# Attention by hash bucket and a gated FFN on one core: one shared hash for two head pairs, another split of the norm's transposes, and one accumulator emptied earlier

## The chip, the cores and the metric

The kernel runs on 1 core of one Trainium2 chip. The metric is device time in microseconds (us). The five engines are TensorE (PE, with its weight loads shown apart as PEld), VectorE (DVE), ScalarE (ACT), GpSimd (POOL) and SyncE (SP), which here only issues DMAs. Each works through its own instructions in order; semaphores tie them together.

## What is computed

```python
def _attn_ref(q, k, v, proj):                      # (4, 8, 768, 64), proj (64, 6)
    q_bits = (np.einsum('bhsd,dk->bhsk', q, proj) > 0)
    k_bits = (np.einsum('bhsd,dk->bhsk', k, proj) > 0)
    q_bucket, k_bucket = ...                        # the 6 bits as one number
    mask = q_bucket[:, :, :, None] == k_bucket[:, :, None, :]
    scores = scale * np.matmul(q, k.transpose(0, 1, 3, 2))
    scores = np.where(mask, scores, -1000000000.0)
    attn = softmax(scores)                          # with 1e-9 added to the sum
    return np.matmul(attn, v)

def _moe_ref(x, w_gate, w_val, w_out, rms_g):       # x: 3072 tokens of 512, d_ff 1536
    xn = x / sqrt(mean(x * x) + 1e-06) * rms_g
    g = xn @ w_gate
    return (g * sigmoid(g) * (xn @ w_val)) @ w_out
```

A query sees only the keys whose six signs agree with its own. The result of the attention, with the heads side by side, goes through an RMS norm and a gated FFN.

## The kernel before

**Units.** The work is cut into 8 units: batch `b` and half of the queries, `u = 2 * b + half`, 384 queries each. A unit has attention for 8 heads, then norm, gate and value matmuls (12 blocks `ft` of the hidden width) and the projection. Heads are prepared in pairs `(b, hp)`, four per batch.

**The mask as rows of the scores.** A pair's q and k are turned so that the 64 dimensions lie on partitions. The hash multiplies them by the projection (`pj`, on PE, in fp32), DVE's `signs` turns the sign bit of each result into plus or minus a constant, and these 6 rows of bits stand below the 64 rows of q and k in the tile `QK` as rows 64 to 69, so that one matmul gives score plus matching term. `hash_direct` (L244) hashes one pair: `hash_pairs` (L230) puts its four sources (k and q of both heads) in four blocks of 32 rows of a bank, one bank for each half `e` of the 768 tokens, `sign` writes them to the tile `bits`, and `send` (L270) has SP copy 6 rows each into `QK` by DMA, four DMAs per pair. `hash_half` (L212) is the other form, used from pair (1, 2) on.

**Steps.** The order of the instructions on every engine is written by a loop over 192 steps `t` (L873 on): scores of step `t + 1` on PE, the exp `probs` of step `t` on ACT, then what `plan[t]` holds. A step is a third of one head. `order` (L590) says which unit and head: units 0 and 1 share the first 48 steps, then 24 steps for each unit. Three steps after its scores a head's weighted sum `av` (L362) runs in two steps; `s_ps` has two buffers, the accumulator `o_ps` of a head pair has one. When a pair of heads is done, `o_step` (`attn_out`, L378) adds the mean term into `otmp` on DVE, which empties `o_ps`, takes the reciprocal, and POOL multiplies into `x` and squares it; `s_step` sums the squares on DVE some steps later.

**Order inside a step.** What is put in with `at` while the loop over `order` runs comes first in its step. A unit's FFN work is spread over the next unit's 24 steps by `spread` (L790), a planner which fills steps by estimated costs (`TURN` 220, `FEED` 324, and so on); it comes after. The list `late` comes behind that. An `o_step` is in `late` unless it falls before step 48 or on place 2 or 4 of a unit's 24 steps.

**The norm.** `norm` (L442) scales the three 128-token thirds of `x` to `xn` in fp16. A third is then turned into `xnT`, either by PE (`turn_x`, L458: four transposes into the bank `x_ps`, then DVE or ACT multiplies by the gain column `gcol`) or by DMA (`turn_dma`, L424, issued by SP; then DVE has put in the gain, as the row `grow`, while scaling). `ONDMA` (L422) says how many thirds of each unit go by DMA. All small PE results (`t_ps`, `d_ps`, `m_ps`, `x_ps`, `g_ps`, `v_ps`, `y_ps`, `z_ps`) share three banks.

**Around the first norm.** Unit 0's last heads end at step 31; its norm, on DVE and POOL, runs in steps 31 to 37. Pair (1, 0) is hashed in step 26 and sent in step 28, pair (1, 1) in steps 32 and 38 (L739 to L743). Dummy matmuls `z_ps` stand in steps 34 to 36. SP has the block loads of pair (1, 2) (`load_blocks`, eight DMAs, and one of V) in step 34 of its queue; the weights come over POOL's queue.

**The tail.** Behind the loop (L883 on): unit 6's projection of thirds 0 and 1, unit 7's norm, the projection of third 2 with unit 7's three turns between its parts, then unit 7's gates, values and projection with nothing else left to overlap.

Of the kernel before, what the change touches and what calls it, by code (L numbers as in the profile page):

```python
# [8 lines left out]
FP32 = mybir.dt.float32  # L9
# [8 lines left out]
S = 768  # L18
D = 64
DMODEL = H * D  # L20
DFF = 1536
NF = DFF // 128
# [11 lines left out]
def kernel(  # L34
# [12 lines left out]
    nc = tc.nc  # L47
    PSUM = bass.MemoryType.PSUM

    const = ctx.enter_context(tc.tile_pool(name="const", bufs=1))  # L50
# [16 lines left out]
    ones_row = nc.const_aps.tensor(1.0, [128, 512], mybir.dt.bfloat16)  # L67
    ones_sq = nc.const_aps.tensor(1.0, [128, 128], mybir.dt.bfloat16)
    praw = const.tile([D, 6], FP32, name="praw")
    pj = const.tile([128, 38], FP32, name="pj")  # L70
    ebias = const.tile([128, 1], FP32, name="ebias")
    mhalf = const.tile([128, 3], FP32, name="mhalf")
    ssp = [const.tile([128, 5, 3], FP32, name=f"ssp{i}") for i in range(2)]
# [60 lines left out]
    KROWS = D + 6  # L134
    qT, kT, QK = {}, {}, {}
# [36 lines left out]
    def turned(b, hp, which):  # L172
        return (qT if which == "q" else kT)[b, hp].rearrange("p (h c) -> p h c", h=2)
# [38 lines left out]
    def hash_half(parts):  # L212

        ps = bank("d_ps", [128, HALF])
        for t, src in parts:
            nc.tensor.matmul(  # L216
                ps[32 * t : 32 * t + 32, :], pj[:, 0:32], src,
                start=True, stop=True, tile_position=(0, 32 * t),
            )
        return ps  # L220
# [6 lines left out]
            op0=ALU.bitwise_and, op1=ALU.bitwise_or,  # L227
        )

    def hash_pairs(srcs):  # L230


        pss = [bank("d_ps", [128, HALF]) for _ in range(2)]
        for t, src in enumerate(srcs):
            for e in range(2):
                nc.tensor.matmul(  # L236
                    pss[e][32 * t : 32 * t + 32, :],
                    pj[64 * e : 64 * e + 64, 6 * e : 6 * e + 32],
                    src[64 * e : 64 * e + 64],
                    start=True, stop=True, tile_position=(64 * e, 32 * t),  # L240
                )
        return pss

    def hash_direct(b, hp, heads):  # L244

        where = [(which, hh) for hh in heads for which in "kq"]
        pss = hash_pairs([turned(b, hp, which)[:, hh, :] for which, hh in where])
        bt = spool.tile([128, S], FP16, name="bits")  # L250

        def sign(e):
            signs(bt[:, e * HALF : (e + 1) * HALF], pss[e])

        def direct(which, e, c0=0, c1=HALF):
            t = where.index((which, heads[0]))
            o = (0 if which == "q" else S) + e * HALF
            signs(
                QK[b, 2 * hp + heads[0], "h"][D:KROWS, o + c0 : o + c1],
                pss[e][32 * t : 32 * t + 6, c0:c1],  # L260
            )

        def move(hh):
            for which in "kq":
                t, o = where.index((which, hh)), 0 if which == "q" else S
                nc.gpsimd.tensor_copy(
                    QK[b, 2 * hp + hh, "h"][D:KROWS, o : o + S], bt[32 * t : 32 * t + 6, :]
                )

        def send(only=heads):  # L270
            for t, (which, hh) in enumerate(where):
                if hh not in only:
                    continue
                o = 0 if which == "q" else S
                nc.sync.dma_start(
                    out=QK[b, 2 * hp + hh, "h"][D:KROWS, o : o + S],
                    in_=bt[32 * t : 32 * t + 6, :],
                )

        return sign, direct, move, send  # L280

    hashed = {}
# [136 lines left out]

    rstds = {}  # L420

    ONDMA = {2: 2, 3: 2, 4: 2, 5: 2, 6: 3}  # L422

    def turn_dma(u, c):  # L424
        if c == 0:
            xnT[u] = npool.tile([128, 4, HALF], FP16, name="xnT", bufs=2)
        nc.sync.dma_start_transpose(  # L427
            out=xnT[u][:, :, c * 128 : (c + 1) * 128], in_=xn[u][:, c, :]
        )
# [12 lines left out]
    def norm(u):  # L442
        if u not in rstds:
            norm_scale(u)
        xn[u] = npool.tile([128, 3, DMODEL], FP16, name="xn")
        for c in range(3 if u else 2):
            if c < ONDMA.get(u, 0):
                nc.vector.scalar_tensor_tensor(
                    out=xn[u][:, c, :], in0=x[u][:, c, :], scalar=rstds[u][:, c : c + 1],
                    in1=grow, op0=ALU.mult, op1=ALU.mult,  # L450
                )
            else:
                norm_third(u, c, nc.vector.tensor_scalar_mul)

    def norm_third(u, c, mul):
        mul(xn[u][:, c, :], x[u][:, c, :], rstds[u][:, c : c + 1])

    def turn_x(u, c, act=False):  # L458
        if c == 0:
            xnT[u] = npool.tile([128, 4, HALF], FP16, name="xnT", bufs=2)  # L460
        ps = bank("x_ps", [128, 4, 128], FP16)
        for kt in range(4):
            nc.tensor.transpose(ps[:, kt, :], xn[u][:, c, kt * 128 : (kt + 1) * 128], ident16)  # L463
        dst = xnT[u][:, :, c * 128 : (c + 1) * 128]
        if act:
            for kt in range(4):
                nc.scalar.mul(dst[:, kt], ps[:, kt], gcol[:, kt : kt + 1])
        else:
            nc.vector.tensor_mul(dst, ps, gcol.unsqueeze(2).to_broadcast([128, 4, 128]))
# [34 lines left out]
    def project(u, c, f0, f1):  # L504
        if f0 == 0:
            obank[u, c] = bank("y_ps")
        y = obank[u, c]
        for ft in range(f0, f1):
            nc.tensor.matmul(  # L509
                y, ht[u][:, ft, c * 128 : (c + 1) * 128], wo[:, ft, :],  # L510
                start=(ft == 0), stop=(ft == NF - 1),
            )
# [6 lines left out]
    def store(u, c):  # L519
        ysb = spool.tile([128, DMODEL], FP32, name="ysb", bufs=3)  # L520
        nc.scalar.copy(ysb, obank.pop((u, c)))  # L521
        nc.sync.dma_start(out=rows_of(u, c), in_=ysb)
# [39 lines left out]
    )  # L562
    for e in range(2):
        rows = slice(64 * e, 64 * e + 64)
        nc.gpsimd.tensor_scalar_mul(pj[rows, 6 * e : 6 * e + 6], praw, -1.0)
    for i in range(2):
        nc.gpsimd.memset(vls[i][:, :, :, 64:65], 1.0)
        nc.gpsimd.memset(vsum[i][:, :, 64:65], 6.0)
# [19 lines left out]
    NS = 24  # L588
# [5 lines left out]
    def at(w, s, f, *a):  # L594
        plan[NS * w + s].append(lambda: f(*a))
# [87 lines left out]
    for hp, ts in ((0, (8, 22, 23, 24, 25, 24, 39, 26, 28, 42)), (1, (20, 27, 28, 29, 30, 29, 41, 32, 33, 43))):  # L683
        tl, ts = ts[0], ts[1:]
        for w in "kq":
            at(0, tl, load_natural, nc.sync, 1, hp, w)
        at(0, tl, load_v, nc.sync, 1, hp)
        at(0, ts[0], new_pair, 1, hp)
        for t, hh, w in zip(ts[0:4], (0, 1, 0, 1), "kkqq"):
            at(0, t, turn_pe, 1, hp, hh, w)  # L690
        at(0, ts[4], cast_pool, 1, hp, "k")
        at(0, ts[5], cast_pool, 1, hp, "q")
        if hp == 0:
            at(0, ts[6], hash_pair, 1, hp)
            at(0, ts[7], send_pair, 1, hp)
        at(0, ts[8], v_prep, 1, hp)
        at(0, ts[8], v_sum, 1, hp)

# [14 lines left out]
    TX = 37  # L713
# [7 lines left out]
    def s_step(u, hp):  # L721
# [3 lines left out]
        else:  # L725
            sumsq(u, hp, sq)

    late = []
    for n, (u, h) in enumerate(order):
        t = 3 * n + 4 - ((u, h) == (0, H - 1))  # L730
        for part in range(2):
            at(0, t + part, av, u, h, part)
        if h % 2:
            if (u, h) == (0, H - 1):

                at(0, t + 1, o_step, u, h // 2, nc.vector)
                at(0, t + 1, norm_scale, u)
                at(0, t + 1, nc.vector.tensor_scalar_mul, gcol, gcol, float(DMODEL) ** 0.5)
                at(0, t + 2, hash_only, 1, 1)  # L739
                at(0, t + 2, hash_signs, 1, 1)  # L740
                at(0, t + 2, norm, u)
                at(0, TX-1, norm_third, u, 2, nc.scalar.mul)
                at(0, TX + 1, send_pair, 1, 1)  # L743
                for c in range(3):
                    at(0, TX, turn_x, u, c, c == 2)
                continue
            if (u, h) == order[-1]:
                at(0, t + 1, o_step, u, h // 2, nc.vector)
                continue

            steps = [(t + 1, o_step), (t + (6 if h < 7 else 3), s_step)]
            for s, step in steps:
                if s < 2 * NS or s % NS in (2, 4):
                    at(0, s, step, u, h // 2)
                else:
                    late.append((s, step, u, h // 2))
# [58 lines left out]
    for u in range(7):  # L815
# [13 lines left out]
        for i in range(9):  # L829
            c, n = divmod(i, 3)  # L830
            steps = [(0, project, u - 1, c, 4 * n, 4 * n + 4)]
# [22 lines left out]
    for (b, hp), (load, kturns, qturns, _) in spots.items():  # L854
# [3 lines left out]
        for w, turns in (("k", kturns), ("q", qturns)):  # L858
            for i, t in enumerate(turns):
                at(0, t, turn_dve, b, hp, w, i, len(turns))  # L860
            t = turns[-1] + 1
# [18 lines left out]
    for t in range(LAST, LAST + 6):  # L880
        for f in plan[t]:
            f()
    for c in range(2):  # L883
        project(6, c, 0, NF)
        store(6, c)
    norm(7)
    project(6, 2, 0, 4)
    for c, f0, f1 in ((0, 4, 6), (1, 6, 8), (2, 8, NF)):
        turn_x(7, c, c == 1)
        project(6, 2, f0, f1)  # L890
    store(6, 2)
    for ft in range(NF):
# [37 lines left out]
```

## Time and profile before

| what | us |
|---|---|
| median of 3 runs | 328.9 (328.4 to 329.17) |
| the profiled execution | 328.83 |
| its span, first to last instruction | 326.7 |
| TensorE busy | 321.3 |
| mean granted TensorE clock | 1.000 |
| ACT exps `psb`, 192 of them | 168.1, mean 0.90 each |
| three DMA transposes of unit 6, issue on SP | 4.63, from 262.17 |
| dummy matmuls `z_ps`, 14 of them | 5.3 |

A line of a timeline gives start and duration in us, engine, line of the kernel, operation, the tiles (out<-in), the shape, how many were merged into the line, and in brackets how long the engine had been idle before it and what ended that. "SPq" is SyncE's own queue: the time is that of issuing, not of the transfer. The chain of waits is followed back from the last instruction to what released it.

### The profile page before, as it was taken

Reading aid. Unit: us, or ns where it says so; the run is one execution under the profiler, and the core shown is the slowest. Engines: PE = TensorE matmul, PEld = TensorE weight load, DVE = VectorE, ACT = ScalarE, POOL = GpSimd, SP = SyncE. Lnnn points to the kernel's source line nnn. Section 1 sums busy time; section 2 is a strip of 40 time slices with the busy share of each in tenths; the row PEclk is TensorE's granted clock in tenths of the full one; section 3 lists DMA queues with packets and bytes.
Section 4 is the critical chain, followed back from the end, with each engine's and each line's share of the span. In section 5 each row is a group of like instructions: output and inputs, shape, how many; then the busy total and the mean of one; then the engine's idle time right before and its main releaser. Section 6 shows DMA issues by size and latency. Waiting matters only on the chain.

```text
span 326.7 us, 7791 instructions
## 1 busy us (share of the span) xinstructions
PE 321.3 (98%) x2955; PEld 194.1 (59%) x2955; DVE 231.2 (71%) x515; ACT 228.3 (70%) x332; POOL 157.6 (48%) x204
## 2 busy tenths in 40 slices
PE   8999999999999999999999999999999999999996
PEld 3576666656565565655566565655666556665554
DVE  5887876859888559874888568885766536675870
ACT  6999887667688667776777677787777767744322
POOL 3999759955974363731873521752682220221000
PEclk9999999999999999999999999999999999999999
DMA  7952999989328828343547047002100040002002
GB/s 216 353 163 69 230 216 200 181 138 182 102 39 155 152 79 154 54 98 99 91 102 141 9 138 135 7 1 69 68 5 3 7 127 14 2 2 90 8 2 96
DMA packets 85741, 32.63 MB, mean 100 GB/s; under 512 B 70908, under 2 KB 82632, under 8 KB 85704
## 3 DMA queue, kind: packets, MB, share of 16 engines
q1 hardware_dynamic: 81800, 27.35, 36.1%
q0 software_dynamic: 3680, 4.72, 8.6%
q8 instruction: 23, 0.38, 0.5%
q14 instruction: 14, 0.11, 0.1%
q10 hardware_dynamic: 224, 0.07, 0.1%
HBM read 28.58 MB, written 6.29 MB: 107 GB/s over the span
## 4 chain that ended last, share of the span: by engine, by line
PE 95%; DMA 2%; ACT 1%; SPq 1%; issue 0%
PE s_ps L345 20%; PE g_ps L480 19%; PE v_ps L480 19%; PE y_ps L509 17%; PE o_ps L370 11%; PE d_ps L216 2%; PE t_ps L156 2%; PE d_ps L236 2%; DMA qn<-in_q_dram 1%; PE x_ps L463 1%; ACT psb L357 1%; PE y_ps L528 1%; DMA xnT<-xn 1%; PE m_ps L329 1%; PE z_ps L576 1%; SPq L427 0%
## 5 line engine op out<-in xcount | busy, mean ns | idle before, releaser
L357 ACT ACTIVATE psb<-s_ps,ebias 128x768 f16<-128x768 f32 x192 | 168.1, 901 | 21.2 <-PE s_ps L345 20.4
L345 PE MATMUL s_ps<-QK 128*128 128x384 f16 (+1 forms) x384 | 93.5, 326 | 1.3 <-ACT psb L357 1.1
L488 ACT ACTIVATE t<-g_ps 128x384 f32<-128x384 f32 x96 | 47.3, 492 | 51.9 <-PE g_ps L480 50.2
L480 PE MATMUL g_ps<-xnT,wg 128*128 128x384 f16 x384 | 82.5, 326 | 0.2 <-DMA xnT<-xn 0.2
L480 PE MATMUL v_ps<-xnT,wv 128*128 128x384 f16 x384 | 81.8, 326 | 0.0
L497 DVE SCALAR_TENSOR_TENSOR a<-t,g_ps 128x384 f32<-128x384 f32 x96 | 53.0, 552 | 28.8 <-ACT t L488 27.3
L391 POOL TENSOR_TENSOR x<-otmp,rcp 128x384 f32<-128x384 f32 x30 | 25.1, 837 | 97.8 <-DVE rcp L389 97.6
L509 PE MATMUL y_ps<-wo,ht 128*128 128x512 f16 x276 | 67.9, 379 | 0.0
L498 DVE SCALAR_TENSOR_TENSOR ht<-a,v_ps 128x384 f16<-128x384 f32 x96 | 53.2, 554 | 12.1 <-PE v_ps L480 4.1
L370 PEld LDWEIGHTS <-psb 128*128 128x128 f16 x1152 | 51.8, 97 | 16.1 <-issue 1.2
L370 PE MATMUL o_ps<-vl,psb 128*128 128x65 f16 x1152 | 55.8, 193 | 0.1
L345 PEld LDWEIGHTS <-QK 128*128 128x128 f16 (+1 forms) x384 | 34.8, 98 | 34.9 <-issue 9.3
L480 PEld LDWEIGHTS <-wg 128*128 128x128 f16 x384 | 35.1, 97 | 21.8 <-issue 0.6
L480 PEld LDWEIGHTS <-wv 128*128 128x128 f16 x384 | 35.1, 97 | 20.7 <-issue 0.2
L509 PEld LDWEIGHTS <-ht 128*128 128x128 f16 x276 | 24.8, 98 | 22.8
L521 ACT COPY ysb<-y_ps 128x512 f32<-128x512 f32 x23 | 13.5, 587 | 17.5 <-PE y_ps L509 17.5
L384 DVE TENSOR_TENSOR otmp<-o_ps,cvb 128x390 f32<-128x390 f32 x32 | 17.9, 558 | 9.8 <-PE o_ps L370 9.8
L208 POOL CAST QK<-qT 64x768 f16<-64x768 f32 x20 | 16.5, 823 | 10.4 <-DVE qT L195 9.5
L397 POOL TENSOR_TENSOR sq<-x 128x384 f32<-128x384 f32 x24 | 19.9, 827 | 1.9
L208 POOL CAST QK<-kT 64x768 f16<-64x768 f32 x20 | 16.4, 822 | 4.6 <-DVE kT L195 2.5
L195 DVE STREAM_TRANSPOSE kT<-kL 128x192 f32<-128x192 f32 x32 | 16.5, 521 | 0.0
L195 DVE STREAM_TRANSPOSE qT<-qL 128x192 f32<-128x192 f32 x32 | 16.3, 526 | 0.0
(85 smaller groups left out, 267.5 us busy)
## 6 DMA issues: line engine op xcount, KB each, us to landing
vn<-in_v_dram SPq DMA_DIRECT2D x16, 384.0 KB
out_dram<-ysb SPq DMA_DIRECT2D x23, 256.0 KB
qL<-in_q_dram SPq DMA_DIRECT2D x40, 96.0 KB
kL<-in_k_dram SPq DMA_DIRECT2D x40, 96.0 KB
kn<-in_k_dram SPq DMA_DIRECT2D x5, 384.0 KB
qn<-in_q_dram SPq DMA_DIRECT2D x5, 384.0 KB
wg<-in_moe_w_gate_dram POOLq DMA_DIRECT2D x2, 768.0 KB, 9.5
wv<-in_moe_w_val_dram POOLq DMA_DIRECT2D x2, 768.0 KB, 11.9
```

The lines of the kernel that those rows point to most:

```text
L195: nc.vector.transpose(dst.rearrange("p (c t r) -> p r c t", c=6, r=4)[:, r], src.rearrange("p (r c) d -> p r c d", r=4)[:, r],)
L208: nc.gpsimd.tensor_copy(QK[b, 2 * hp + hh, "h"][0:64, o : o + S], src[64 * hh : 64 * hh + 64, :])
L345: nc.tensor.matmul(ps[:, j, 0:HALF], QK[b, h, "h"][rows, S + jt * 128 : S + (jt + 1) * 128], QK[b, h, "h"][rows, half * HALF : (half + 1) ...
L357: nc.scalar.activation(psb[u, h][:, 2 * ch : 2 * ch + 2, :], sps.pop((u, i))[:, :, 0:HALF], AF.Exp, bias=ebias, scale=ESCALE,)
L370: nc.tensor.matmul(o[:, c, hh, 0:65], psb[u, h][:, jt, c * 128 : (c + 1) * 128], vls[b % 2][:, h, 2 * (jt % 3) + jt // 3 if b in PARITY el ...
L391: eng.tensor_mul(xd.rearrange("p c (h d) -> p c h d", h=2), tmp[:, :, :, 0:64], r.to_broadcast([128, 3, 2, 64]),)
L397: eng.tensor_mul(sq, xd, xd)
L480: nc.tensor.matmul(ps, w[:, kt, fs], xnT[u][:, kt, :], start=(kt == 0), stop=(kt == 3))
L488: nc.scalar.activation(t, fbank[u, ft, "g_ps"], AF.Tanh, scale=0.5)
L497: nc.vector.scalar_tensor_tensor(out=a, in0=t, scalar=1.0, in1=g, op0=ALU.add, op1=ALU.mult)
L498: nc.vector.scalar_tensor_tensor(out=ht[u][:, ft, :], in0=a, scalar=0.5, in1=vv, op0=ALU.mult, op1=ALU.mult)
L509: nc.tensor.matmul(y, ht[u][:, ft, c * 128 : (c + 1) * 128], wo[:, ft, :], start=(ft == 0), stop=(ft == NF - 1),)
```

## The change

It has four parts.

1. Pairs (1, 0) and (1, 1) are hashed together in step 32, and both are sent in step 38; the hash in step 26 and the send in step 28 are gone. `hash_pairs` takes several sets of sources. Both sets use the same two banks and the same blocks of 32 rows: the first pair's matmuls start the accumulation and the second pair's add to it, with the weights shifted by 6 columns, so that the second pair's bits come in rows 6 to 11 of each block. For that `pj` gets 6 more columns of zeros, and `hash_half` takes its window 6 columns on.
2. Unit 6 turns two thirds by DMA instead of three, and its last third on PE, placed by the planner. Unit 7 turns its first third by DMA instead of none; its last third is scaled by ACT, and of its two turns on PE the second is now the one that ACT multiplies. Unit 7's norm stands ahead of the projection of unit 6's second third.
3. The `o_step` of unit 6's second head pair, in step 158, comes ahead of the planner's work of that step.
4. Unit 7's sums of squares come two steps sooner (four steps after the head's `av` begins, not six).

```diff
-        pss = [bank("d_ps", [128, HALF]) for _ in range(2)]
-        for t, src in enumerate(srcs):
-            for e in range(2):
-                nc.tensor.matmul(
-                    pss[e][32 * t : 32 * t + 32, :],
-                    pj[64 * e : 64 * e + 64, 6 * e : 6 * e + 32],
-                    src[64 * e : 64 * e + 64],
-                    start=True, stop=True, tile_position=(64 * e, 32 * t),
-                )
+        pss = [bank("d_ps", [128, HALF]) for _ in range(2)]
+        for n, srcs in enumerate(sets):
+            for t, src in enumerate(srcs):
+                for e in range(2):
+                    nc.tensor.matmul(
+                        pss[e][32 * t : 32 * t + 32, :],
+                        pj[64 * e : 64 * e + 64, 6 * (e + 1 - n) : 6 * (e + 1 - n) + 32],
+                        src[64 * e : 64 * e + 64],
+                        start=(n == 0), stop=(n == len(sets) - 1),
+                        tile_position=(64 * e, 32 * t),
+                    )
...
-        pss = hash_pairs([turned(b, hp, which)[:, hh, :] for which, hh in where])
+        pairs = hp if isinstance(hp, tuple) else (hp,)
+        pss = hash_pairs(*([turned(b, i, which)[:, hh, :] for which, hh in where] for i in pairs))
...
+            for n, i in enumerate(pairs):
+                for t, (which, hh) in enumerate(where):
+                    if hh not in only:
+                        continue
+                    o, r = 0 if which == "q" else S, 32 * t + 6 * n
+                    nc.sync.dma_start(
+                        out=QK[b, 2 * i + hh, "h"][D:KROWS, o : o + S],
+                        in_=bt[r : r + 6, :],
+                    )
...
-    ONDMA = {2: 2, 3: 2, 4: 2, 5: 2, 6: 3}
+    ONDMA = {2: 2, 3: 2, 4: 2, 5: 2, 6: 2, 7: 1}
...
-        for c in range(3 if u else 2):
+        for c in range(3 if 0 < u < 7 else 2):
...
-        if hp == 0:
-            at(0, ts[6], hash_pair, 1, hp)
-            at(0, ts[7], send_pair, 1, hp)
...
+    AHEAD = {(6, 1)}
...
-                at(0, t + 2, hash_only, 1, 1)
-                at(0, t + 2, hash_signs, 1, 1)
+                at(0, t + 2, hash_only, 1, (0, 1))
+                at(0, t + 2, hash_signs, 1, (0, 1))
...
-                at(0, TX + 1, send_pair, 1, 1)
+                at(0, TX + 1, send_pair, 1, (0, 1))
...
-            steps = [(t + 1, o_step), (t + (6 if h < 7 else 3), s_step)]
+            steps = [(t + 1, o_step), (t + (3 if h == 7 else 4 if u == 7 else 6), s_step)]
             for s, step in steps:
-                if s < 2 * NS or s % NS in (2, 4):
+                if s < 2 * NS or s % NS in (2, 4) or (step is o_step and (u, h // 2) in AHEAD):
...
-    for c in range(2):
-        project(6, c, 0, NF)
-        store(6, c)
+    project(6, 0, 0, NF)
+    store(6, 0)
     norm(7)
+    norm_third(7, 2, nc.scalar.mul)
+    turn_dma(7, 0)
+    project(6, 1, 0, NF)
+    store(6, 1)
     project(6, 2, 0, 4)
-    for c, f0, f1 in ((0, 4, 6), (1, 6, 8), (2, 8, NF)):
-        turn_x(7, c, c == 1)
+    for c, f0, f1 in ((1, 4, 8), (2, 8, NF)):
+        turn_x(7, c, c == 2)
         project(6, 2, f0, f1)
     store(6, 2)
```

More of the change, by code (lines that the diff above doesn't have):

```diff
@@ L69 @@
     praw = const.tile([D, 6], FP32, name="praw")
-    pj = const.tile([128, 38], FP32, name="pj")
+    pj = const.tile([128, 44], FP32, name="pj")
     ebias = const.tile([128, 1], FP32, name="ebias")
@@ L216, in hash_half @@
             nc.tensor.matmul(
-                ps[32 * t : 32 * t + 32, :], pj[:, 0:32], src,
+                ps[32 * t : 32 * t + 32, :], pj[:, 6:38], src,
                 start=True, stop=True, tile_position=(0, 32 * t),
@@ L228, in signs, with hash_pairs @@
         )
-    def hash_pairs(srcs):
+    def hash_pairs(*sets):
         pss = [bank("d_ps", [128, HALF]) for _ in range(2)]
-        for t, src in enumerate(srcs):
-            for e in range(2):
-                nc.tensor.matmul(
-                    pss[e][32 * t : 32 * t + 32, :],
-                    pj[64 * e : 64 * e + 64, 6 * e : 6 * e + 32],
-                    src[64 * e : 64 * e + 64],
-                    start=True, stop=True, tile_position=(64 * e, 32 * t),
-                )
+        for n, srcs in enumerate(sets):
[8 more added lines that the diff above has]
+                    )
         return pss
@@ L263, in move @@
         def move(hh):
+            assert len(pairs) == 1
             for which in "kq":
@@ L270, in send @@
         def send(only=heads):
[L271 to L278, printed above, removed]
+            for n, i in enumerate(pairs):
[7 more added lines that the diff above has]
+                    )
         return sign, direct, move, send
@@ L564 @@
         rows = slice(64 * e, 64 * e + 64)
-        nc.gpsimd.tensor_scalar_mul(pj[rows, 6 * e : 6 * e + 6], praw, -1.0)
+        nc.gpsimd.tensor_scalar_mul(pj[rows, 6 * e + 6 : 6 * e + 12], praw, -1.0)
     for i in range(2):
```

## The prediction

> **What bounds the kernel now.** I read the page first (busy times and the chain that ended last), then the waits of TensorE, and then the timeline around each place that the diff touches. Page, busy time and chain:
>
> ```profile
> PE 321.3 (98%) x2955; PEld 194.1 (59%) x2955; DVE 231.2 (71%) x515; ACT 228.3 (70%) x332; POOL 157.6 (48%) x204
> PE 95%; DMA 2%; ACT 1%; SPq 1%; issue 0%
> ```
>
> TensorE (PE) sets the time: any PE work or PE hole taken away before the end shortens the run by as much, as long as no other wait moves in. DVE, ACT, POOL and the DMA queues matter only where PE waits for them. The list of waits shows few:
>
> ```profile
> PE s_ps L345 <- ACT psb L357: 1.1, 2, 0.8
> PE g_ps L480 <- DMA xnT<-xn: 0.2, 1, 0.2
> ```
>
> It understates them, because a matmul's record lasts longer than it holds the array. In the chain a pair of `s_ps` matmuls steps on by 0.33, four `g_ps` by 0.65, four `y_ps` by 0.86, nine `o_ps` by 0.27. I use these steps to find holes: start of the next group, minus start of this one, minus its step. In the timeline (start, duration, engine, line, operation, tiles, form, count) four places have such holes:
>
> ```profile
> 241.07 0.49 PE L345 MATMUL s_ps<-QK 128*128 128x384 f16 x2
> 241.68 0.43 PE L370 MATMUL o_ps<-vl,psb 128*128 128x65 f16 x9
> ...
> 262.17 4.63 SPq L427 DMA_TRANSPOSE xnT<-xn  x3
> ...
> 267.46 0.49 PE L345 MATMUL s_ps<-QK 128*128 128x384 f16 x2
> 268.16 0.81 PE L480 MATMUL g_ps<-xnT,wg 128*128 128x384 f16 x4 [0.22 <-DMA xnT<-xn]
> ```
>
> Unit 6, head 4: 241.68-241.07-0.33 = 0.28 us, PE waits for the single `o_ps` bank, which DVE's `otmp` (240.97, 0.56 long) empties. First gate of unit 6: 268.16-267.46-0.33 = 0.37, PE waits for the last of three DMA transposes (the chain has it issued at 265.58 and landed 2.45 later, at 268.03). Four microseconds on, the chain runs through ACT: its exp `psb` at 271.30 ends at 272.20 and frees the bank for `s_ps` at 272.25, while PE's `v_ps` x4 from 271.31 were through at 271.96: 0.28 again. ACT was late there because its tanh (`t`, 269.01) waited for that late gate, with the exps queued behind it.
>
> The tail and the first norm:
>
> ```profile
> 297.60 0.39 PE L463 MATMUL x_ps<-ident,xn 128*128 128x128 f16 x4
> 297.82 0.59 PE L509 MATMUL y_ps<-wo,ht 128*128 128x512 f16 x2
> ...
> 298.68 1.15 ACT L467 ACTIVATE xnT<-x_ps,gcol 128x128 f16<-128x128 f16 x4 [1.16 <-PE x_ps L463]
> ...
> 299.13 1.03 PE L509 MATMUL y_ps<-wo,ht 128*128 128x512 f16 x4
> 300.08 0.82 PE L480 MATMUL g_ps<-xnT,wg 128*128 128x384 f16 x4
> ```
>
> ```profile
> 38.31 0.49 PE L345 MATMUL s_ps<-QK 70*128 70x384 f16 x2
> 38.73 0.51 PE L236 MATMUL d_ps<-kT,pj 64*32 64x384 f32 x2
> 39.08 0.49 PE L236 MATMUL d_ps<-kT,pj 64*32 64x384 f32 x2
> 39.54 0.93 PE L345 MATMUL s_ps<-QK 70*128 70x384 f16 x4
> ```
>
> Four `x_ps` transposes cost PE 297.82-297.60 = 0.22. The first gate of unit 7 comes 300.08-299.13-0.86 = 0.09 late. One hash of a pair holds PE from 38.64 (38.31+0.33) to 39.54: 0.90, in two fp32 passes 0.35 apart (38.73, 39.08) plus 0.09 to enter and 0.46 for the last pass and the way out.
>
> **Part 1, the shared hash.** It leaves step 26 (32.65 to 33.6: 0.90 of PE, two `bits` instructions of 0.51 on DVE, two banks) and makes the hash at step 32 longer: 8 matmuls more, two passes of 0.35, so 0.69 more. DVE's two `bits` there stay two. Of the 0.90 that PE gains at step 26 only about 0.74 arrives: ACT's exps run without a gap until the one that ends at 33.81, and the next but one `s_ps` (34.57) needs its bank, so it can start at 33.83 at best. From there to 38.64 PE has no hole, so step 32 starts 0.74 earlier and ends 0.69 later: -0.05. Behind it, until the first gate at 44.79, ACT paces (exps 0.8 apart, its share of the norm, its four `xnT`), so the norm on DVE, 0.74 earlier, gains nothing. Bounds: -0.2 (a whole entry and exit saved) and +0.16 (nothing saved, 0.90-0.74). I take **-0.05**, the row of the two passes being the nearest.
>
> The Trainium skill, "TensorE: Matmul & The Clock Gate", section "The mechanism", says that weight loads overlap matmuls in flight only when they go to other rows of the array; the second pair's weights go to the same rows, and by that the sum of this part would be +0.16. The trace speaks against it in part: all 16 weight loads of this hash start by 38.80, those of the second pass while the first pass still runs in the same rows (38.73 to 39.08).
>
> **Part 2, the bits' transfers.** Pair (1,0)'s four sends leave SP at 34.79 and are now queued at step 38, behind the eight block loads and the V load of pair (1,2):
>
> ```profile
> 30.62 0.41 SPq L106 DMA_DIRECT2D vn<-in_v_dram  x1
> 34.79 2.84 SPq L275 DMA_DIRECT2D QK<-bits  x4
> 37.73 11.10 SPq L120 DMA_DIRECT2D qL<-in_q_dram  x4
> 48.87 8.89 SPq L120 DMA_DIRECT2D kL<-in_k_dram  x4
> 57.86 0.58 SPq L106 DMA_DIRECT2D vn<-in_v_dram  x1
> 58.55 2.99 SPq L275 DMA_DIRECT2D QK<-bits  x4
> ```
>
> SP stood still from 31.04 to 34.79 for those bits; now the blocks are issued from 31.1, 6.6 earlier. They crawl because the weights share the DMA engines (share 1.31, 218 GB/s in 44 to 50): one block load takes about 5.9. So they run about 1.2 loads ahead, the eighth lands where the seventh did (59.1 by the trace's completion records, against 62.8), V is issued near 56.7 and the eight sends from 57.4, 0.7 each. The first scores of batch 1 (62.75, the first `s_ps` of form 128*128) need the first two. Behind V's 384 KB I put their landing at 60 to 62: hidden, **0**, margin about 1. Without that lead they land like (1,1)'s two first sends did, 66.03 and 66.80: +4.05. Queued behind the sends are pair (1,3)'s loads, now from about 63 instead of 61.63; DVE's turns of them are near 75, their last block landed at 71: nothing. The weights (gate half at 39.7, value half at 44.0) are first read at 44.79 and 45.44, and moved no slower beside the blocks (218 GB/s in all) than before them (206 in 38 to 41.5): nothing.
>
> **Part 3, the earlier `otmp`.** In step 158 it now stands before that step's gate and value. Its `o_ps` is complete at 238.96, DVE is free from 238.59 to 239.84, so it ends at 239.55 instead of 241.53, delays no other DVE work, and the hole of **0.28** at 241.68 goes (bounds -0.28 and 0). POOL's multiply after it is queued behind the same casts as before.
>
> **Part 4, unit 6.** Two thirds by DMA: the second lands where it does now, one issue (1.3) sooner, 266.7, over 1 us before the gate. The last third costs PE four transposes, +0.22, in step 176 near 266.6, and DVE one `xnT` of 0.69 from 267.0 to 267.7, where DVE idled 3.37 before 266.80; behind it `otmp` slips from 266.80 to 267.7, read by PE's `o_ps` only at 269.3. Gone: 0.37 for the DMA. Recomputing the order that the planner gives, one half gate slides from step 178 to 179, so ACT's tanh of it comes after the next exp instead of before: that exp no longer waits for the gate, and the hole of 0.28 at 272.25 goes. -0.37+0.22-0.28 = **-0.43** (bounds -0.43 and +0.22, if both waits are replaced).
>
> **Part 5, unit 7.** Sums of squares two steps sooner: the last one (292.21, 0.55 long) leaves the place before `otmp` (292.67), so the norm is 0.46 earlier, rstd near 295.5. The first third is scaled by 296.25 (0.75), its DMA issued at 296.3 and landed 2.45 later, 298.8; even with the slowest of the trace (first of unit 6: issued 262.17, landed 265.33, 3.17) 299.5. The gate comes at 300.08-0.22-0.09 = 299.77, so hidden; with the old norm time it would be 299.2 to 299.9. Behind the transpose on SP stands one store, which nobody awaits. The ACT third (0.73, from 295.5) is done before ACT's `ysb` at 296.93. New on the path: ACT's four `xnT` (1.15) now belong to the last third, 299.1 to 300.27; the gate's fourth matmul, due at 300.26, waits some 0.05 for the fourth. -0.31+0.05 = about **-0.25** (bounds -0.31, and +0.2 if the gate waits for all four).
>
> **Sum.** -0.05+0-0.28-0.43-0.25 = -1.01. The profiled execution took 328.83 (span 326.7), the median is 328.9: **327.9**.
>
> **Rivals.** 0.2% (0.66) is about what can be told from no change.
> (a) The forecast: 55%, own range 327.4 to 328.3.
> (b) The ACT waits stay: the exp at 272 is late for another reason (it has 0.28), and the tail's ACT `xnT` hold all of the gate (0.25). For it: both rest on ACT, which has 70% load; against it: at the first norm the gate started at 44.79, before the fourth ACT `xnT` ended (45.0). -0.48, 328.4: 20%.
> (c) Slower: the rows of pair (1,0) land after 62.75, PE stands at the first scores of batch 1, nothing behind can be pulled ahead. For it: the same queue gave (1,1)'s rows 7.5 after their issue; against it: the 6.6 head start. It is a loss from 1.0 late, at 63.8; at (1,1)'s landing -1.01+4.05, 331.9; halfway 329.9: 13%.
> (d) The second pair's weights are not loaded ahead and the shared hash saves nothing: +0.21 on the sum, 328.1: 12%.
>
> Faster by 0.2% (under 328.24): nearly all of (a), two thirds of (d), a third of (b): 0.66. Slower (over 329.56): two thirds of (c): 0.09. Same: 0.25. The range, 327.3 to 329.3, leaves out the worse half of (c) and a little below (a).
>
> **What would show it.** Right: no hole at head 4 of unit 6, no PE wait on `xnT` at unit 6's first gate, `s_ps` three steps later without ACT before it, one `d_ps` group of 32 records lasting about 1.6, the tail's first gate 0.3 earlier than the rest. Wrong: a PE wait on DMA `QK<-bits` near 62.7, a `d_ps` group of 1.8, or a gate of unit 7 that waits for DMA or for ACT's `xnT`.

## The result and the profile after

The kernel after takes 329.63 us (median of 20, 328.71 to 333.42), the kernel before 328.65 (median of 20, 327.74 to 329.23): a ratio of 1.0052, 95% interval 1.0032 to 1.0072. It is slower by half a per cent in the mean (330.43 against 328.67) and by 0.3% in the median, as seven long executions pull the mean up; 327.9 was forecast. The profiled execution took 333.02 (span 331.2), near the upper end.

Busy times, chain and the row of the scores on the page after (columns of the row: line, engine, operation, tiles, count, then busy time and mean, then the idle time before and what ended most of it):

```profile
PE 322.6 (97%) x2954; PEld 195.5 (59%) x2955; DVE 230.0 (69%) x512; ACT 228.2 (69%) x333; POOL 157.3 (47%) x204
...
PE 95%; DMA 2%; ACT 1%; DVE 1%; issue 0%; SPq 0%; DVEq 0%
...
L351 PE MATMUL s_ps<-QK 128*128 128x384 f16 (+1 forms) x384 | 93.7, 327 | 5.0 <-DMA QK<-bits 3.8
```

DVE has lost its two `bits` and is 1.2 us less busy, but TensorE is busy 1.3 us longer with one matmul record fewer (part of it at half clock, below), and it has waited 3.8 us for the bits' transfers. The list of waits of TensorE after (us in total, times, longest):

```profile
PE s_ps L351 <- DMA QK<-bits: 3.8, 1, 3.8
```

The 0.2 for `xnT` is gone, and a single wait has come that is larger than all that the change can gain. Its place, in TensorE's timeline, and SyncE's queue and POOL's weight load beside it:

```profile
62.39 0.49 PE L486 MATMUL v_ps<-xnT,wv 128*128 128x384 f16 x2
66.63 0.80 PE L351 MATMUL s_ps<-QK 128*128 128x384 f16 x2 [3.75 <-DMA QK<-bits]
```

```profile
31.16 12.48 SPq L120 DMA_DIRECT2D qL<-in_q_dram  x4
43.74 13.83 SPq L120 DMA_DIRECT2D kL<-in_k_dram  x4
57.66 0.58 SPq L106 DMA_DIRECT2D vn<-in_v_dram  x1
58.35 8.11 SPq L281 DMA_DIRECT2D QK<-bits  x8
```

```profile
57.04 0.82 POOL L587 DMA_DIRECT2D wo<-in_moe_w_out_dram  x1
```

The blocks leave 6.6 us earlier than before (31.16 against 37.73), yet V leaves only 0.2 earlier (57.66 against 57.86). The first two sends land at 66.32 and 66.50 by the trace's completion records, 8.0 and 7.3 us after their issue, and TensorE stands at the first scores of batch 1 from 62.71 (62.39 + 0.32) to 66.63: 3.92 us.

The wait costs more than itself. The windows of the kernel after (stretch and its length, then busy time with count of PE, PEld, DVE, ACT and POOL, granted clock, DMA share, GB/s):

```profile
62.70:66.60 3.90, 0.18 (x2) 0.00 (x0) 1.66 (x3) 1.17 (x2) 3.68 (x6) 0.98 0.66 149
66.60:68.00 1.40, 1.37 (x12) 0.93 (x13) 0.00 (x0) 0.00 (x0) 0.29 (x1) 0.50 0.03 8
...
71.00:73.00 2.00, 2.00 (x19) 1.10 (x18) 1.94 (x4) 1.84 (x3) 0.00 (x0) 1.00 0.91 143
```

Behind the hole the granted clock is 0.50; the clock's own record has it so from 66.45 to 69.86. Comparing the start of the same matmul in the two traces, the kernel after is 0.04 ahead at 60, 3.88 behind at 62.8, and 5.28 behind from 72.8 on: 3.92 for the wait and 1.40 for the half clock. From there it makes up 0.98 at the places of the forecast and 0.12 at a gate near 193 us, loses 0.33 at a hash near 203 (last section), and ends 4.53 behind.

### The profile page after: what moved, and what is told of

The parts are those of the page before. It is cut to its first block, busy times and chain, and to the rows that moved or that the text cites. A ratio compares the mean times of both kernels' runs of the same rounds, so it can differ in the third digit from the quotient of the medians.

```text
span 331.2 us, 7785 instructions
## 1 busy us (share of the span) xinstructions
PE 322.6 (97%) x2954; PEld 195.5 (59%) x2955; DVE 230.0 (69%) x512; ACT 228.2 (69%) x333; POOL 157.3 (47%) x204
## 4 chain that ended last, share of the span: by engine, by line
PE 95%; DMA 2%; ACT 1%; DVE 1%; issue 0%; SPq 0%; DVEq 0%
PE s_ps L351 20%; PE g_ps L486 18%; PE v_ps L486 18%; PE y_ps L515 18%; PE o_ps L376 10%; PE d_ps L216 2%; PE t_ps L156 2%; DMA QK<-bits 2%; PE d_ps L238 2%; PE z_ps L582 1%; PE x_ps L469 1%; PE y_ps L534 1%; PE m_ps L335 1%; ACT psb L363 1%; DVE a L503 0%; PE s_ps L156 0%
## 5 line engine op out<-in xcount | busy, mean ns | idle before, releaser
L494 ACT ACTIVATE t<-g_ps 128x384 f32<-128x384 f32 x96 | 47.1, 491 | 56.7 <-PE g_ps L486 56.7
L475 DVE TENSOR_TENSOR xnT<-x_ps,gcol 128x512 f16<-128x512 f16 x11 | 7.4, 688 | 15.7 <-PE x_ps L469 15.6
```

Of the source, the lines that this page charges most:

```text
L494: nc.scalar.activation(t, fbank[u, ft, "g_ps"], AF.Tanh, scale=0.5)
```

## The experiments

The theory: the sends of pair (1,0), now queued behind nine more issues of SyncE, land too late, and all else in the change is worth what the sum said. The rival: the shared hash itself costs. The first four kernels were compared with 23 runs of the kernel before (median 328.76), the second four with 23 others (328.70).

### The sends before the key blocks

```diff
-        at(0, load, load_blocks, nc.sync, b, hp)
+        if (b, hp) == (1, 2):
+            at(0, load, load_blocks, nc.sync, b, hp, "q")
+            load = TX + 1
+            at(0, load, load_blocks, nc.sync, b, hp, "k")
+        else:
+            at(0, load, load_blocks, nc.sync, b, hp)
```

`load_blocks` takes only the named blocks; V follows the key blocks.

> The changed kernel with one thing moved: pair (1,2)'s k blocks and V are issued by SP behind the eight sends, its q blocks stay ahead of them. Theory 1 (the loss is the place of pair (1,0)'s sends in SP's queue, behind nine loads that crawl beside the weights): the sends are issued from about 44, as soon as the q blocks are, land near 57, and the first scores of batch 1 find their rows there; no PE wait on QK<-bits, TensorE at full clock throughout, the other parts' -1.0 is left: about 327.7, -0.3% against before. Theory 2 (the shared hash itself, with its later bits and 32 records, makes the loss): the wait stays, 329.6 or more. A miss of both: the k blocks come late to DVE's turns near 64 and the wait moves there.

Measured: 328.13 (12 runs), ratio 0.9983, 0.9974 to 0.9993. (1,0)'s rows land from 52.42 to 54.33 and the wait at 62.7 is gone. A smaller one has come; SyncE's queue and TensorE's timeline of this kernel:

```profile
42.47 14.49 SPq L283 DMA_DIRECT2D QK<-bits  x8
57.01 7.03 SPq L122 DMA_DIRECT2D kL<-in_k_dram  x4
...
79.95 5.74 SPq L312 DMA_DIRECT2D QK<-bits  x8
```

```profile
81.61 0.81 PE L488 MATMUL v_ps<-xnT,wv 128*128 128x384 f16 x4
83.15 0.48 PE L353 MATMUL s_ps<-QK 128*128 128x384 f16 x2 [0.73 <-ACT psb L365]
```

The eight sends held SyncE for 14.5 us, and what is queued behind them slipped, down to the next pairs' eight sends at 79.95. The second of those lands at 83.02, and that releases the weight load at 83.04 for the scores at 83.15: a hole of 0.89 (83.15 - 81.61 - 0.65). The bracket names ACT, whose signal came last by 0.08, but with (1,0)'s sends alone ahead of the key blocks (below) the same scores start at 82.78 while that exp is still running (82.72 to 83.62), so it isn't what they wait for. So it is the first fault again, smaller and 20 us later.

### Everything but the shared hash

```diff
+        if hp == 0:
+            at(0, ts[6], hash_pair, 1, hp)
+            at(0, ts[7], send_pair, 1, hp)
...
-                at(0, t + 2, hash_only, 1, (0, 1))
-                at(0, t + 2, hash_signs, 1, (0, 1))
+                at(0, t + 2, hash_only, 1, 1)
+                at(0, t + 2, hash_signs, 1, 1)
...
-                at(0, TX + 1, send_pair, 1, (0, 1))
+                at(0, TX + 1, send_pair, 1, 1)
```

> The changed kernel without its first part: pairs (1,0) and (1,1) hashed and sent as before, the other three parts kept. If those parts bring what their holes in the trace of before were worth (0.28 at unit 6's head 4, 0.44 at unit 6's gate, 0.26 in the tail): 0.98 less than before, about 327.7, ratio 0.997. The rival, that they bring less than they seem to in the changed kernel's trace because a stall there had shifted the phases: 328.2 or more.

Measured: 327.55 (6 runs), ratio 0.9966, 0.9953 to 0.9978. The earlier `otmp` and units 6 and 7 give what they were costed at: 0.96, where the interval is 0.7 to 1.5. (Its profile has a hole of its own, 0.9 us before a gate at 155.59, whose DMA transpose lands at 155.46. Why that one was late there was not pursued.)

### Nothing but the late sends

The kernel before, hash in step 26 and all, with one line moved:

```diff
-            at(0, ts[7], send_pair, 1, hp)
+            at(0, TX + 1, send_pair, 1, hp)
```

> The kernel before with one thing moved: pair (1,0) is hashed in step 26 as before, but its four sends stand in step 38, behind pair (1,2)'s loads and ahead of pair (1,1)'s sends. Theory 1: the same wait as in the changed kernel, 1 to 4 us at the first scores of batch 1 (more where the clock drops), so 329.6 to 333. Theory 2 (it takes the shared hash): within 0.3 of before.

Measured: 331.32 (6 runs, 329.67 to 334.9), ratio without the longest 1.0068, 1.0046 to 1.0090. Its timeline of TensorE and one window:

```profile
64.97 0.48 PE L345 MATMUL s_ps<-QK 128*128 128x384 f16 x2 [2.40 <-POOL sq L397]
```

```profile
66.40:68.80 2.40, 2.40 (x9) 1.13 (x8) 0.99 (x2) 0.96 (x2) 0.20 (x1) 0.50 0.87 135
```

The two sends land at 63.76 and 64.83, the hole is 2.56 us, and half clock follows here too, from 65.41 to 68.82. (The bracket names POOL, whose signal came last by 0.14; the weight load of these scores is released by the second send.) With the old hash untouched the loss is all there: the rival has fallen.

### V behind the sends

```diff
-        at(0, load, load_v, nc.sync, b, hp)
+        at(0, TX + 1 if (b, hp) == (1, 2) else load, load_v, nc.sync, b, hp)
```

> The changed kernel with pair (1,2)'s V load (384 KB) issued behind the eight sends instead of ahead of them; the eight block loads stay ahead. It parts theory 1 in two. 1a (the sends wait for V's data in the same ring): they start when the blocks are through, near 59, land by 61.5, no wait, 327.7. 1b (a transfer of SP takes some 4 us to start while the weights' queue is busy, whatever stands ahead): issued from 57.7, they land at 62.5 to 64, a wait of 0 to 1.3, 327.7 to 329.

Measured: 328.53 (12 runs), ratio 0.9996, 0.9986 to 1.0006. The sends leave at 57.60 and 58.42 and land at 63.02 and 63.38, still 5 us later; the hole is 0.88 and the clock stays at 0.999:

```profile
63.52 0.48 PE L351 MATMUL s_ps<-QK 128*128 128x384 f16 x2 [0.72 <-POOL vsum L327]
```

That is theory 1b. So V ahead of them is only part of the delay: the second send lands 3.1 us sooner than in the first profile of the kernel after (66.50), 1.7 and 0.5 sooner than in two later ones (65.08 and 63.91, below). Something else makes a send of 9 KB take 5 us.

### Half of the sends before the key blocks

SyncE's order becomes: query blocks, (1,0)'s four sends, key blocks and V, (1,1)'s four sends.

```diff
-                at(0, TX + 1, send_pair, 1, (0, 1))
+                at(0, TX + 1, send_of, (0,))
...
-        at(0, load, load_blocks, nc.sync, b, hp)
-        at(0, load, load_v, nc.sync, b, hp)
+        if (b, hp) == (1, 2):
+            at(0, load, load_blocks, nc.sync, b, hp, "q")
+            at(0, TX + 1, load_blocks, nc.sync, b, hp, "k")
+            at(0, TX + 1, load_v, nc.sync, b, hp)
+            at(0, TX + 1, send_of, (1,))
+        else:
+            at(0, load, load_blocks, nc.sync, b, hp)
+            at(0, load, load_v, nc.sync, b, hp)
```

> The kernel after with SyncE's order of issues in the first norm changed to: pair (1,2)'s four query blocks, the four sends of pair (1,0)'s rows, the four key blocks and V, the four sends of pair (1,1)'s rows. Theory (the eight sends are late because they stand behind twelve issues of SyncE, the last of them V, and the rest of the change is worth its 0.98 us): SyncE issues the first four sends between 42.5 and 46 us, (1,0)'s rows land before 55, TensorE has no wait on them at 62.7 and no half clock behind it; the key blocks are issued about 3 us later than in the kernel after, not 14 as when all eight sends stood ahead, so the 0.9 us hole at 83 us of that run does not come. 327.6, ratio 0.997. Rival (any send ahead of the key blocks makes SyncE stand for the signs, and unit 2 pays for it): a wait of 0.5 to 0.9 us before 85 us, 328.1 to 328.5. Rival (the shared hash itself costs 4 us): 332.

Measured: 327.55 (5 runs, 327.39 to 327.67), ratio 0.9961, 0.9947 to 0.9974. This is the full gain with the shared hash in, and it beats both kernels. SyncE's queue, and TensorE at the place of the wait:

```profile
31.19 12.19 SPq L122 DMA_DIRECT2D qL<-in_q_dram  x4
43.49 7.22 SPq L285 DMA_DIRECT2D QK<-bits  x4
50.76 6.65 SPq L122 DMA_DIRECT2D kL<-in_k_dram  x4
57.51 0.58 SPq L106 DMA_DIRECT2D vn<-in_v_dram  x1
58.14 2.98 SPq L285 DMA_DIRECT2D QK<-bits  x4
```

```profile
62.42 0.49 PE L490 MATMUL v_ps<-xnT,wv 128*128 128x384 f16 x2
62.74 0.49 PE L355 MATMUL s_ps<-QK 128*128 128x384 f16 x2
```

The four sends land from 55.72 to 56.69, later than the 55 expected, but six microseconds ahead of need. Putting them in costs V nothing: it leaves at 57.51, 0.15 earlier than in the kernel after. The next pairs' second send lands at 80.92 (83.02 in the first experiment), and the hole at 83 does not come.

### The shared hash alone

That order of issues in the kernel before, with the shared hash and without the other three parts.

> The kernel before with the shared hash and SyncE's order of the run before this one (query blocks, the sends of (1,0), key blocks and V, the sends of (1,1)), and without the earlier otmp and the changes of units 6 and 7. Theory: the shared hash is worth next to nothing by itself once its rows are in time: 0.05 us by the sum (328.7, ratio 0.9998, so within 0.2% of the kernel before); in the trace TensorE's events from 30 us on are 0.7 us ahead at first, as in the kernel after, and 0.05 ahead by 60. Rival (sharing rows makes each second set of weights wait for the matmuls before it): 0.16 us slower. Rival (the order of issues costs something in unit 2): 0.5 to 0.9 us slower, with a wait of TensorE before 85 us.

Measured: 328.46 (12 runs), ratio 0.9990, 0.9979 to 1.0001. Within 0.2%, as the sum has it: TensorE's events are 0.08 ahead of the kernel before from 41 to 140. At its end it is 0.49 ahead, which neither the sum nor the shared hash accounts for. 0.14 of that comes at a gate at 192.8, and 0.30 at unit 6's first gate, with the old three transposes by DMA: SyncE issued them in 4.43 us here, against 4.63 in the profile before, and the hole of 0.37 there is 0.09. In the experiment that only moved the sends they took 4.17 and there was no hole. The 12 runs bear the 0.49 out: from first to last instruction they are 0.50 shorter in the mean than the 23 of the kernel before (326.37 against 326.87), with 0.14 more of time outside that span (2.13 against 1.99).

### The sends by GpSimd's queue

```diff
-                at(0, TX + 1, send_pair, 1, (0, 1))
+                at(0, TX + 1, send_of, (0,), nc.gpsimd)
+                at(0, TX + 1, send_of, (1,))
```

> The kernel after with the four sends of pair (1,0)'s rows issued by GpSimd, at the same step, and those of (1,1) by SyncE as in the kernel after. It tells the place in SyncE's queue apart from the traffic of the weights: GpSimd is idle from 42 to 45.7 us, but its DMA queue holds the weights that are loading until about 53 us, and the rows go behind them. Theory (the place in the queue decides): the rows land before 56 us, no wait at 62.7 and none at 83: 327.6, ratio 0.997. Rival (the transfers are slow whatever queue carries them while weights load): a wait at 62.7 stays, of 1 to 3.9 us.

Measured: 327.94 (11 runs), ratio 0.9976, 0.9966 to 0.9986. The rows land from 52.43 to 52.94, no wait at 62.7 and none at 83. They left at 41.46 to 43.17 and took 10 to 11 us, so they are slow on this queue too, as the rival has it; the early issue is what brings them in time. The median stands 0.4 above the other order's, but from first to last instruction only 0.1 (325.8 against 325.7); the rest is time outside that span (2.11 in the mean, against 1.87).

### The weights out of the way

```diff
-        at(0, 39 + 3 * i, load_w, wo, moe_w_out, 6 * i, 6)
+        at(0, 39 + 8 * i, load_w, wo, moe_w_out, 6 * i, 6)
```

The second half of `wo`, 768 KB, is issued by POOL in step 47, no longer in step 42.

> The kernel after with the load of wo's second half moved from step 42 to step 47, so that the weights' queue carries nothing between about 59 us and the landing of the rows. Theory that the load of weights, not the order alone, sets the last 5 us of the sends' way: V lands near 60.5 and the first sends by 61.5 to 62, so the wait at 62.7 is gone or under 0.5 us and the half clock with it; wo's half is then late itself, and TensorE waits some 3 us for it at the first output projection near 68: 329 to 332. Rival (the transfers behind V take 4 to 5 us whatever else runs): the rows land near 66 as before, the wait of 3.9 us stays, and wo costs on top: 333 or more.

One execution, profiled: 335.6. SyncE, POOL's load and TensorE in its timeline:

```profile
56.57 1.02 SPq L106 DMA_DIRECT2D vn<-in_v_dram  x1
57.69 5.82 SPq L281 DMA_DIRECT2D QK<-bits  x8
```

```profile
64.49 0.89 POOL L587 DMA_DIRECT2D wo<-in_moe_w_out_dram  x1
```

```profile
62.72 0.49 PE L351 MATMUL s_ps<-QK 128*128 128x384 f16 x2
...
73.06 2.72 PE L515 MATMUL y_ps<-wo,ht 128*128 128x512 f16 x6 [5.58 <-DMA wo<-in_moe_w_out_dram]
```

In the same place of the queue, behind V, the sends now land at 60.51 and 60.70, 2.8 and 2.2 us after their issue, and the wait at 62.7 is gone. V itself lands at 60.48, 3.9 us after its issue, where it took 8.1 in the kernel after (57.66 to 65.78). `wo` is late instead: 5.6 us, not the 3 expected, so the time is above the 329 to 332 of the theory and where the rival put it, but the landings go with the theory. The other part of the delay is `wo`'s second half, which in the kernel after is issued at 57.04 and landed at 66.14, right over V and the sends.

### The kernel after, twice more

> The kernel after as it is, profiled once more. Of its 20 timed executions 7 took 331.3 to 333.4 us at a mean granted clock of 0.994 or 0.995, and 13 took 328.7 to 330.1 at 0.999 or 1.0. Theory: the wait for (1,0)'s rows differs from execution to execution, and where it is long the half clock behind it adds 1.4 us more. An execution of the first kind shows again a wait of some 3.9 us and the clock at 0.50 for 3.4 us, near 333; one of the second kind shows a wait of about 1.5 to 2 us at the same place (329.3 less 327.66 by the sum) and no halved clock. Rival (the wait is always 3.9 us and the second kind gains elsewhere): a wait of 3.9 us at a time below 330.

> As the run before this one, a third profile of the kernel after, since each profile is one draw of the two kinds of execution. Theory: the time less 327.66 us equals the wait of TensorE for (1,0)'s rows, with 1.4 us more where the clock shows 0.50 behind it. Rival: the time goes elsewhere too, and the two differ by over 0.5 us.

One execution each: 329.98 and 328.85. The waits of TensorE in the one and in the other:

```profile
PE s_ps L351 <- DMA QK<-bits: 1.8, 1, 1.8
```

```profile
PE s_ps L351 <- DMA QK<-bits: 1.4, 1, 1.4
```

Neither shows a halved clock. The second send lands at 65.08 and 63.91 (66.50 in the first profile). Time less 327.66, the forecast for a kernel without the wait, is 2.32 and 1.19; the waits are 1.79 and 1.37. The first differs by 0.53, a little over the 0.5 that the rival named, and the traces show where: TensorE is 0.57 behind the kernel before at 28 us already in the one, 0.17 ahead in the other.

So the wait does differ between executions. V lands at 65.78, 64.56 and 60.73 in the three profiles, in the first two less than 1 us ahead of the second send; in the third the sends still took 5.5 us, though V was through at 60.73. What makes V's landing differ is not shown. The seven executions of 331.3 to 333.4 are by their granted clock (0.994 or 0.995) those with a wait that was long enough for the half clock; one of them was profiled. Time less 327.66 and 1.4 puts their waits at 2.2 to 4.4, an estimate; the median of 329.63 stands for a wait of about 2.

## Why the prediction was wrong

**The failed step** is in Part 2: "Behind V's 384 KB I put their landing at 60 to 62: hidden", with a margin of about 1. The second of them landed at 66.50, 65.08 and 63.91 in three profiles, and the term put at 0 was a wait of 1.4 to 3.9 us, with 1.4 more for the half clock where it was long. Rival (c) was this case, with its place, at 13%; its 331.9 held no half clock, and the profiled execution took 333.02.

Two things went into that step. The smaller is the head start, put at "about 1.2 loads" (6.6 over 5.9 is 1.1). By the completion records the lead is 5.4 us at the first block (43.09 against 48.45 before), 4.3 at the second, 2.5 at the third and 0.5 at the fourth (56.89 against 57.42). Up to about 57 the weights hold both kernels' blocks back; then the blocks that are left land within a few microseconds in either (in the trace of before at 57.42, 58.22, 58.82 and 59.12, where I reckoned with 5.9 a block). So SyncE got to V at 57.66, 1.0 later than the 56.7 put down. This alone did not decide: in the third profile V left at 56.92 and the sends from 57.60, all but as forecast, and they landed at 63.09 and 63.91.

The larger is the transfer of the sends themselves. I reckoned V ahead of them, and not `wo`'s second half, which stands in the trace of before too, issued at 57.11 and landed at 66.39. The only row of before that had sends beside that load is the one in my rival, (1,1)'s, 7.5 us from issue to landing. (1,0)'s own sends of before, beside an earlier load of weights, took 6.0 and 5.6 for the first two (34.79 to 40.82, 35.54 to 41.12); from 57.4 and 58.1 that is 63.4 and 63.7, past 62.75 too. I gave the one row to the rival, left the other out, and used for the forecast an estimate that no row stood for. With the load moved, the same sends landed at 60.51 and 60.70, 2.2 to 2.8 us after their issue; so 60 to 62 would have been right without it.

**Part 1** was right: the hash of 32 matmuls holds TensorE for 1.54 us (from the last score matmul ahead of it, at 37.79, to the first behind it, at 39.50, less that one's 0.17), 0.64 over one pair's 0.90 where 0.69 was put down. TensorE is 0.69 ahead before it (0.74 put down) and 0.04 ahead at 60. By the rule of the Trainium skill that I set beside it ("TensorE: Matmul & The Clock Gate", "The mechanism"), it would have been 0.16 behind; the trace does not bear that out, and rival (d) falls with it. In the chain of after:

```profile
38.11 1.45 PE d_ps L238 x32
```

**Parts 3 to 5** were right to 0.02 in the profiled execution: -0.28 at head 4 of unit 6, -0.44 by unit 6's later gates (forecast -0.43), -0.26 in the tail (-0.25). Timeline of after:

```profile
267.40 3.57 SPq L433 DMA_TRANSPOSE xnT<-xn  x2
...
271.83 0.39 PE L469 MATMUL x_ps<-ident,xn 128*128 128x128 f16 x4
...
273.24 0.81 PE L486 MATMUL g_ps<-xnT,wg 128*128 128x384 f16 x4
...
274.48 0.90 ACT L363 ACTIVATE psb<-s_ps,ebias 128x768 f16<-128x768 f32 x1
```

```profile
301.47 1.22 SPq L433 DMA_TRANSPOSE xnT<-xn  x1
...
303.90 1.14 ACT L473 ACTIVATE xnT<-x_ps,gcol 128x128 f16<-128x128 f16 x4 [1.59 <-PE x_ps L469]
304.56 0.85 PE L486 MATMUL g_ps<-xnT,wg 128*128 128x384 f16 x4
```

The gate at 273.24 waits for no transfer, the exp at 274.48 follows without a gap, and the last gate takes 0.85 for 0.81, about the 0.05 that the fourth ACT `xnT` was to cost. Rival (b) falls. One price in Part 4 is less sure than it looked: the 0.37 gained at unit 6's first gate is the wait of one execution. Two kernels with the old three transposes had 0.09 and nothing there, so beside those the change of unit 6 gives next to nothing: 0.28 and 0.09 at most, less the 0.22 of the matmuls, so 0.06 to 0.15.

The parts add up: the kernel without the shared hash and the one with (1,0)'s sends moved both stand at 327.55, against 327.80 and 327.69 from the sum (328.76 - 0.96 and 328.70 - 1.01). From first to last instruction, without the time around that span, their medians are 0.95 and 1.20 shorter than those of the kernel before.

## What to carry to other kernels

When a transfer is moved down a queue, price it by the row that had the same kind of transfer under the same traffic, and list every load that is in flight at its new time, those on other queues too; here the row that was kept for the rival was the one that belonged in the sum. A head start on a queue that other traffic holds back is not worth its microseconds: look where the last transfer lands, not where the first leaves. And before giving up an edit that loses, try the order of the issues: four sends between the query and the key blocks turned 0.5% lost into 0.4% gained.

## What the runs showed of the hardware

**A small transfer beside a weight load.** The first two sends of 9 KB near 58 us landed 2.2 to 2.8 us after their issue with the weights' queue idle (one execution), and 5.0 to 8.0 us after it while 768 KB of weights ran on another queue (the kernels before and after, and those with only the sends late and with V behind them). The Trainium skill, "DMA: Bandwidth & Descriptors", section "Queues, rings and completion order", says that each DMA engine takes turns between the queues that have work for it, a packet at a time. The trace agrees in kind: from 44 to 50 us of the kernel after SyncE's queue and the weights' moved 786 and 784 packets, but 0.10 and 1.18 MB; for SyncE's block loads that is 17 GB/s.

**The half clock after a short wait.** Holes of TensorE of 3.92 and 2.56 us came with 3.41 us at a granted clock of 0.50, from 0.2 before their end and 0.4 behind it; one of 5.6 with 6.83, 2.7 of them inside the hole. Holes of 1.96, 1.54 (1.79 and 1.37 in the list of waits, which counts from the end of the record before) and 0.88 came with none. The price jumps with it: where the hole of the kernel after is 1.96, TensorE falls back by 1.8 us against the kernel before (from 0.50 to 2.31 behind), and where it is 3.92, by 5.3. Where between 1.96 and 2.56 the step lies, and whether it is always at the same length, is not shown.

**A hash that takes a pass more.** In the three profiles of the kernel after (and in three of the experiments: the sends before the key blocks, V behind the sends, the weights out of the way) a hash near 203 takes three fp32 passes, not two, and costs 0.3. In the first profile its last turn of queries on DVE ends at 207.91, after the hash has begun at 207.63. Where the same turn ends in time (202.19 against 202.29, with (1,0)'s sends moved) it takes two. In all six with three passes DVE stands idle for 0.46 to 0.47 us ahead of an `ht` shortly before that turn, where the ones with (1,0)'s sends moved have 0.10; in the third profile both signals that this `ht` waits for had come by 201.49, and it starts at 201.96. What holds it the profile does not show.
